# Turning normalised rows through DRAM and DVE's 32x32 transposes in place of PE's transposes, in a four-layer attention and MLP kernel

## Chip, cores and metric

The kernel runs on one core of one Trainium2 chip. The metric is the device time of one execution in microseconds, lower is better. The kernel before takes 2529.15 us, the median of three runs (2528.08 to 2529.36).

## The reference

Four blocks run one after the other on 2048 rows of 576 numbers, all float32: attention A, MLP B, attention A, MLP B, with the same weights both times. Each adds its result to the rows, and each begins with a LayerNorm of the rows.

```python
def _A_ref(x, wqkv, w_phi, wo):
    q, k, v = ...                      # x @ wqkv, in 32 heads of 18
    phi_q = concatenate([softmax(q @ w_phi), softmax(-(q @ w_phi))])
    phi_k = concatenate([softmax(k @ w_phi), softmax(-(k @ w_phi))])
    kv = einsum("bhsf,bhsd->bhfd", phi_k, v); z = einsum("bhsf->bhf", phi_k)
    num = einsum("bhqf,bhfd->bhqd", phi_q, kv)
    den = einsum("bhqf,bhf->bhq", phi_q, z)[..., None] + 1e-6
    return (num / den) ... @ wo

def _B_ref(x, w1, b1, w2, b2):         # w1: 576 x 4608, w2: 4608 x 576
    h = relu(x @ w1 + b1)
    return (h * h) @ w2 + b2

x = x + _A_ref(layernorm(x), ...)
x = x + _B_ref(layernorm(x), ...)
x = x + _A_ref(layernorm(x), ...)
x = x + _B_ref(layernorm(x), ...)
```

## The kernel before

**Blocks and tiles.** The 2048 rows are cut into four blocks (`NB`) of 512 rows (`TB`), and a block into four tiles of 128 rows (`NT`). The matmuls contract over the 576 features, so the normalised rows are needed with the features on the partitions: four chunks of 128 features (`KC`) and a rest of 64 (`DT`). Float32 values are split into a high part in fp32r and the difference, so that a product is three passes: an array `xh` holds the high part, `xl` the low part of the four full chunks, and the fifth chunk of `xh` holds the high part of the rest on one half of the partitions and its low part on the other half.

**The MLP loop.** `g_mlp` (L759) runs one block through the MLP: for each of 36 slices `f` of 128 hidden features, `hidden(f)` (L808) is 14 matmuls into the PSUM bank `h` (L824), `square(f)` (L826) makes ReLU and square on ACT (L829, L830) and splits the result on DVE (L833, L834), and `second(f - 1)` (L852) is 15 matmuls into five accumulators (L849, L841). There is one bank `h`, so `hidden(f + 1)` can only start when the ReLU of `f` has read it. In the first block of the first layer the weights are split and stored to DRAM (`fresh`, L784 to L797); in the other seven blocks they are loaded in split form, 640 KB (L787) and 576 KB (L799) for each `f`, into two buffers each. So a load of `f + 1` is issued when the matmuls of `f - 1` have let go of its buffer.

**What is woven in.** `g_mlp` yields after each `hidden` and each `second`, and `weave` (L92) then runs one slot of a `Plan` (L101): the attention of the next block, and in the first layer also keys and values of the block just finished. `plan.put(turn, depth, ...)` gives slot `round(2 * turn) + 1`, so whole turns lie behind a `second`, half turns behind a `hidden`; within a slot the larger depth comes first. After the first two `hidden`, slots 2 and 3 follow one another with nothing between them, behind `second(0)`.

**The norm.** `Norm` (L327) works on a tile `t` in steps: `stats` (L353, on DVE, and the inverse root on GpSimd), `scale` (L365: two DVE instructions, 512 and 64 columns, into `xn` and `xd`; in the attention of a block `then` also adds a bias to the rows and stores them to `xm`, L693 and L694), `turn` (L377: four PE transposes into a PSUM bank at L386, then ACT copies the high part at L387 and DVE makes the low part at L388), and `rest` (L390: for two tiles together two PE transposes of the 64 columns, L395, and an ACT and a DVE instruction, L396 and L397). `plan_norm` (L696) puts these steps into a plan. It is called in `plan_attend` (at L755), six times in all, and in `plan_keys` (at L1349), three times, all in the first layer. The opening, the barrier at the start of a layer and `between` the layers use `Norm` with steps of their own.

**Who orders what.** The instructions of PE, ACT, DVE and GpSimd run in the order of the program text (L1131 and L1386, `ordered`). SP, which issues every DMA, is not in that list: the framework orders its queue by its own estimate of when each DMA is ready. Whatever the order, SP issues one after the other, and a DMA that waits holds those behind it.

Of the kernel before, what the change touches and what calls it, by code (L numbers as in the profile page):

```python
# [7 lines left out]
F32 = mybir.dt.float32  # L8
F32R = mybir.dt.float32r
AF = mybir.ActivationFunctionType  # L10
ALU = mybir.AluOpType
AX = mybir.AxisListType

P = 128
TB = 512
NT = TB // P
# [5 lines left out]
def layers_kernel(  # L22
# [18 lines left out]
    nc = tc.nc  # L41
    S, D = x_in.shape[1], x_in.shape[2]
# [3 lines left out]
    out = out.rearrange("o s d -> (o s) d")  # L46
    NB = S // TB
    NF = F // P
    KC = D // P
    DT = D - KC * P  # L50
# [13 lines left out]
    sb = ctx.enter_context(tc.tile_pool(name="sb", bufs=2))  # L64
    ps_w = ctx.enter_context(tc.tile_pool(name="ps_w", bufs=2, space=bass.MemoryType.PSUM))
    ps_a = ctx.enter_context(tc.tile_pool(name="ps_a", bufs=1, space=bass.MemoryType.PSUM))
    dram = ctx.enter_context(tc.tile_pool(name="dram", bufs=1, space=bass.MemoryType.DRAM))

    xs = [[dram.tile([P, D], F32, name=f"xs{b}_{t}") for t in range(NT)] for b in range(NB)]
    xm = [[dram.tile([P, D], F32, name=f"xm{b}_{t}") for t in range(NT)] for b in range(NB)]  # L70
    xth = [dram.tile([P, NC * TB], F32, name=f"xth{b}") for b in range(NB)]
    xtl = [dram.tile([P, KC * TB], F32, name=f"xtl{b}") for b in range(NB)]
    dense1 = [dram.tile([P, 2 * NC * P], F32, name=f"dw1_{f}") for f in range(NF)]
# [6 lines left out]
    def wtile(name):  # L80
        n = len(spare["tags"])
        spare["i"] += 1
        i = spare["i"] % (n + 2)
        if i < n:
            return ps_a.tile([P, TB], F32, tag=spare["tags"][i], name=name)
        return ps_w.tile([P, TB], F32, tag="w", name=name)
# [14 lines left out]
    class Plan:  # L101

        def __init__(self):
            self.at = {}
# [64 lines left out]
    class Fold:  # L169
# [38 lines left out]
        def turn(self, k):  # L208
            c, i = divmod(k, 3)
            if i == 0:  # L210
                self.folds[c] = sb.tile([P, 2 * D], F32R, tag="wraw" if c in (2, 3) else "hb", name=f"ff{c}")
            w, n = gw[self.batches[i][0][1]], len(self.batches[i])
            pt = wtile(f"fp{c}_{i}")
            for j, (h, g) in enumerate(self.batches[i]):
                a = h * D + g * GW
                nc.tensor.transpose(pt[:w, j * P : (j + 1) * P], self.raws[c][:, a : a + w], ident)
            wt = self.wts[k] = sb.tile([GW, TB], F32, tag="ft", name=f"ft{c}_{i}", bufs=4)
            if i == 0:
                nc.vector.tensor_copy(wt[:w, : n * P], pt[:w, : n * P])
            else:  # L220
                nc.scalar.activation(wt[:w, : n * P], pt[:w, : n * P], AF.Copy)
# [82 lines left out]
    def asked(which, name, tags=TAGS_A):  # L304

        pair, calls = [], []

        def ask(half, k):
            if k == 0:
                pair.append(piece_tiles(f"{name}{which}{half}", tags))  # L310
            for d, piece in moved(which, half, k, pair[half][k]):
                nc.sync.dma_start(piece, d)

        return pair, [lambda half=half, k=k: ask(half, k) for half in range(2) for k in range(2)]
# [8 lines left out]
    def xt_tiles(name):  # L323
        return {"h": sb.tile([P, NC, TB], F32R, tag="xh", name=f"{name}h"),
                "l": sb.tile([P, KC, TB], F32R, tag="xl", name=f"{name}l")}

    class Norm:  # L327
# [37 lines left out]
        def scale(self, t):  # L365
            name = self.name
            x, (mv, rstd) = self.x.pop(t), self.stat.pop(t)
            if self.xd is None:
                self.xd = sb.tile([P, NT, DT], F32, tag="xd", name=f"{name}e", bufs=1)
            xn = sb.tile([P, KC * P], F32, tag="xn", name=f"{name}n{t}")  # L370
            nc.vector.tensor_scalar(xn, x[:, : KC * P], mv[:, 0:1], rstd, op0=ALU.subtract, op1=ALU.mult)
            nc.vector.tensor_scalar(self.xd[:, t], x[:, KC * P :], mv[:, 0:1], rstd, op0=ALU.subtract, op1=ALU.mult)
            if self.then:
                self.then(t, x)
            self.xn[t] = xn
# [14 lines left out]
        def rest(self, h):  # L390
            xh = self.dst["h"]
            rows = slice(h * TB // 2, (h + 1) * TB // 2)
            pt = wtile(f"{self.name}p{NT}{h}")
            for i in range(NT // 2):
                nc.tensor.transpose(pt[:DT, i * P : (i + 1) * P], self.xd[:, h * NT // 2 + i], ident)  # L395
            nc.scalar.activation(xh[:DT, KC, rows], pt[:DT, : TB // 2], AF.Copy)  # L396
            nc.vector.tensor_sub(xh[DT:, KC, rows], pt[:DT, : TB // 2], xh[:DT, KC, rows].bitcast(F32))  # L397

    XT = (("h", xth, 0, KC // 2), ("l", xtl, 0, KC // 2), ("h", xth, KC // 2, NC), ("l", xtl, KC // 2, KC))

    def xt_part(b, x, i):
        n, d, c0, c1 = XT[i]
        return d[b][:, c0 * TB : c1 * TB], x[n][:, c0:c1].rearrange("p c n -> p (c n)").bitcast(F32)

    def spill(b, x, parts=range(4)):
        for i in parts:
            d, piece = xt_part(b, x, i)
            nc.sync.dma_start(d, piece)
# [44 lines left out]
    def make_raw(x, t, pair, name):  # L453
        raw = new_raw(t, name)
        for half in range(2):
            half_raw(x, t, pair, half, raw, name)
        return raw
# [21 lines left out]
    def exponents(raw, name):  # L479
        mm = peaks(raw, name)  # L480
        e = new_e(name)
        for s in range(2):
            difference(raw, mm, e, s, nc.vector)
        return e
# [8 lines left out]
    def totals(e, r):  # L493
        exponential(e)
        normalisers(e, r)
# [197 lines left out]
            nc.vector.tensor_add(x, x, b2t)  # L693
            nc.sync.dma_start(xm[self.b][t], x)  # L694

    def plan_norm(plan, norm, x_of, stats, scales, turns, rests, late=()):  # L696
        for t in range(NT):
            plan.put(stats[t], 0, lambda t=t: norm.stats(t, x_of(t)))
            plan.put(scales[t], 1, norm.scale, t)
            plan.put(turns[t], -1 if t in late else 2, norm.turn, t)  # L700
        for h in range(2):
            plan.put(rests[h], 2, norm.rest, h)
# [35 lines left out]
    def plan_attend(plan, at, gap, layer, b, raws, dst, name, o, queries=None):  # L738

        out = Out(layer, b, [], name)  # L740
        out.pair, calls = o
        if queries:
            for t in range(NT):
                plan.put(at + gap * t, 0, queries, t)
            at += 1
        for n, call in enumerate(calls):
            plan.put(at + n, 9, call)
        at = plan_queries(plan, at, gap, layer, raws, [], out.ph, name) + 1
        for i in range(2 * NG):
            plan.put(at + i / 2, 0, out.turn, i)  # L750
            plan.put(at + (i + 1) / 2, 1, out.times, i)
        at += NG + 1
        for t in range(NT):
            plan.put(at + t - 1, 9, out.load, t)
        plan_norm(plan, Norm(dst, f"{name}n", out.keep), out.project, [at + t for t in range(NT)],  # L755
                  [at + 1, at + 2, at + 4, at + 5], [at + 4 + t for t in range(NT)], [at + 5, at + 7])


# [585 lines left out]
    def plan_keys(plan, prev_rows, last, keep):  # L1344

        pb, done = prev_rows
        m = f"1_{pb}"
        xk, es, ks, vts = {}, {}, {}, {}
        plan_norm(plan, Norm(xk, f"n{m}"), lambda t: done[t], (0, 0, 1, 2), (1, 1, 2, 3), (2, 3, 4, 4.5), (3, 5), (3,))  # L1349
        (vw, vcalls), (kw, kcalls) = asked("v", f"w{m}"), asked("k", f"w{m}", TAGS_C)  # L1350
        for n in range(4):
            plan.put(8 + n if last else 2 + n / 2, 9, vcalls[n])
            plan.put(n / 2, 9, kcalls[n])
        if not last:
            for n in range(4):
                plan.put(5 + n / 2, -1, lambda n=n: spill(pb, xk, [n]))

        def keys(t):
            ks[t] = make_raw(xk, t, kw, f"k{m}k")

        def values(t):
            vts[t] = make_v(xk, t, vw, f"v{m}")

        def soft1(t):
            es[t] = exponents(ks.pop(t), f"k{m}K{t}")

        def soft2(t):
            r = sb.tile([P, 2, H], F32, tag="r", name=f"k{m}K{t}r")
            totals(es[t], r)
            scaled(es[t], r)  # L1370

        def add(t):
            kv_tile(1, vts.pop(t), es.pop(t), f"kv{m}_{t}")

        for t in range(NT):
            plan.put(4 + t, 0, keys, t)
            plan.put(5 + t, 1, soft1, t)
            plan.put(6 + t, 2, soft2, t)
            if not last:
                plan.put(4.5 + t, 0, values, t)  # L1380
                plan.put(8.5 + t // 2 * 2, 3, add, t)
        if last:
            keep.update(x=xk, es=es, v=vw, k=kw)
        return 11.5
# [25 lines left out]
```

## Time and profile before

| | |
|---|---|
| median of three runs | 2529.15 us |
| the profiled execution: its time, its span | 2530.61 us, 2528.9 us |
| ACT busy | 741.9 us, 29% of the span |
| granted TensorE clock | 1.000 |
| DMA moved | 505.48 MB, 200 GB/s over the span |
| DMAs issued by SP for the weights in split form (L787, L799) | 252 of each |

The span runs from the first to the last instruction. "Busy" is the time that an engine works on an instruction; a wait is not busy. The chain of waits follows the work that ended last back to the start, at each step to what released it, and so shows who set the end. The trace of the profile can be asked for stretches of time, for lines of the kernel and for who waited for whom. Of DMAs it shows when SP issued them and what waited for them; the share of the 16 DMA engines that was busy is given for a stretch.

### The profile page before, as it was taken

Reading aid. Unit: us, or ns where it says so; the run is one execution under the profiler, and the core shown is the slowest. Engines: PE = TensorE matmul, PEld = TensorE weight load, DVE = VectorE, ACT = ScalarE, POOL = GpSimd, SP = SyncE. Lnnn points to the kernel's source line nnn. Section 1 sums busy time; section 2 is a strip of 40 time slices with the busy share of each in tenths; the row PEclk is TensorE's granted clock in tenths of the full one; section 3 lists DMA queues with packets and bytes.
Section 4 is the critical chain, followed back from the end, with each engine's and each line's share of the span. In section 5 each row is a group of like instructions: output and inputs, shape, how many; then the busy total and the mean of one; then the engine's idle time right before and its main releaser. Section 6 shows DMA issues by size and latency. Waiting matters only on the chain.

```text
span 2528.9 us, 37324 instructions
## 1 busy us (share of the span) xinstructions
PE 2512.7 (99%) x15300; PEld 2215.4 (88%) x15300; DVE 1166.8 (46%) x1986; ACT 741.9 (29%) x1268; POOL 113.4 (4%) x275
## 2 busy tenths in 40 slices
PE   9999999999999999999999999999999999999999
PEld 8998888888888988888888988888888888888887
DVE  6887955434634446345113775332353326332112
ACT  5544443322222222223223332222222222222221
POOL 4302000000000000000000010000000000000000
PEclk9999999999999999999999999999999999999999
DMA  9514887867647576484665345457544665456565
GB/s 318 174 53 138 288 280 259 309 216 265 214 148 261 179 262 213 147 272 147 196 198 168 115 142 189 152 192 258 183 161 155 221 231 164 148 187 230 195 193 174
DMA packets 161288, 505.48 MB, mean 200 GB/s; under 512 B 21350, under 2 KB 49798, under 8 KB 161118
## 3 DMA queue, kind: packets, MB, share of 16 engines
q1 hardware_dynamic: 161118, 503.10, 59.8%
q8 instruction: 121, 1.98, 0.3%
q14 instruction: 49, 0.40, 0.0%
HBM read 418.39 MB, written 84.64 MB: 199 GB/s over the span
## 4 chain that ended last, share of the span: by engine, by line
PE 97%; DMA 1%; DVE 1%; ACT 0%; issue 0%; SPq 0%; DVEq 0%; ACTq 0%
PE m_1ph L824 9%; PE m_3ph L824 9%; PE m_0ph L824 9%; PE m_2ph L824 9%; PE m_1acc L849 7%; PE m_3acc L849 7%; PE m_2acc L849 7%; PE m_0acc L849 7%; PE m_1acc L841 2%; PE m_3acc L841 2%; PE m_2acc L841 2%; PE m_0acc L841 2%; PE a_2po L686 1%; PE a_0po L686 1%; PE kvp L527 1%; PE a_3po L686 1%
## 5 line engine op out<-in xcount | busy, mean ns | idle before, releaser
L824 PE MATMUL m_2ph<-a_2nh,m_2h 128*128 128x512 f32 x720 | 225.4, 395 | 2.1 <-DMA m_2h<-dw 2.1
L824 PE MATMUL m_0ph<-a_0nh,m_0h 128*128 128x512 f32 x720 | 226.3, 396 | 0.2 <-DMA m_0h<-dw 0.2
L849 PE MATMUL m_3acc<-m_3s,m_3hb 128*128 128x448 f32 x864 | 189.7, 367 | 0.3 <-DVE m_3hb L833 0.3
L849 PE MATMUL m_0acc<-m_0s,m_0hb 128*128 128x448 f32 x864 | 189.9, 368 | 0.0
L849 PE MATMUL m_1acc<-m_1s,m_1hb 128*128 128x448 f32 x864 | 189.4, 367 | 0.3 <-PE m_1ph L824 0.3
L849 PE MATMUL m_2acc<-m_2s,m_2hb 128*128 128x448 f32 x864 | 189.6, 367 | 0.0
L849 PEld LDWEIGHTS m_1acc<-m_1s,m_1hb 128*128 128x128 f32 x864 | 161.5, 188 | 18.2 <-PE m_1ph L824 0.5
L833 DVE CAST m_2hb<-m_2hr 128x512 fp32r<-128x512 f32 x72 | 30.8, 427 | 317.8 <-ACT m_2hr L830 317.4
L849 PEld LDWEIGHTS m_3acc<-m_3s,m_3hb 128*128 128x128 f32 x864 | 161.2, 188 | 17.8 <-PE m_3ph L824 0.5
L849 PEld LDWEIGHTS m_2acc<-m_2s,m_2hb 128*128 128x128 f32 x864 | 160.7, 188 | 16.1
L849 PEld LDWEIGHTS m_0acc<-m_0s,m_0hb 128*128 128x128 f32 x864 | 160.3, 188 | 15.6
L824 PEld LDWEIGHTS m_2ph<-a_2nh,m_2h 128*128 128x128 f32 x720 | 135.3, 188 | 32.8 <-issue 2.5
L824 PEld LDWEIGHTS m_0ph<-a_0nh,m_0h 128*128 128x128 f32 x720 | 135.3, 188 | 30.5 <-issue 0.6
L833 DVE CAST m_1hb<-m_1hr 128x512 fp32r<-128x512 f32 x72 | 30.7, 427 | 269.2 <-ACT m_1hr L830 269.2
L829 ACT ACTIVATE m_2hr<-m_2ph,b1t 128x512 f32<-128x512 f32 x72 | 49.6, 689 | 353.7 <-PE m_2ph L824 353.7
L833 DVE CAST m_0hb<-m_0hr 128x512 fp32r<-128x512 f32 x72 | 30.8, 427 | 260.8 <-ACT m_0hr L830 255.2
L829 ACT ACTIVATE m_0hr<-m_0ph,b1t 128x512 f32<-128x512 f32 x72 | 49.6, 689 | 334.3 <-PE m_0ph L824 334.3
L829 ACT ACTIVATE m_1hr<-m_1ph,b1t 128x512 f32<-128x512 f32 x72 | 49.6, 689 | 323.2 <-PE m_1ph L824 323.2
L829 ACT ACTIVATE m_3hr<-m_3ph,b1t 128x512 f32<-128x512 f32 x72 | 49.6, 689 | 240.3 <-PE m_3ph L824 240.3
L824 PE MATMUL m_3ph<-t0onh,m_3h 128*128 128x512 f32 (+1 forms) x380 | 113.3, 385 | 0.7 <-ACT t0onh L387 0.5
L833 DVE CAST m_3hb<-m_3hr 128x512 fp32r<-128x512 f32 x72 | 30.7, 426 | 180.5 <-ACT m_3hr L830 180.5
L824 PE MATMUL m_1ph<-t1onh,m_1h 128*128 128x512 f32 (+1 forms) x380 | 113.2, 385 | 0.6 <-ACT t1onh L387 0.5
(1934 smaller groups left out, 5618.8 us busy)
## 6 DMA issues: line engine op xcount, KB each, us to landing
m_2h<-dw SPq DMA_DIRECT2D x72, 640.0 KB
m_0h<-dw SPq DMA_DIRECT2D x72, 640.0 KB
m_1h<-dw SPq DMA_DIRECT2D x72, 640.0 KB
m_2s<-dw SPq DMA_DIRECT2D x72, 576.0 KB
m_0s<-dw SPq DMA_DIRECT2D x72, 576.0 KB
m_1s<-dw SPq DMA_DIRECT2D x72, 576.0 KB
dw<-m_3h SPq DMA_DIRECT2D x36, 640.0 KB
m_3h<-dw SPq DMA_DIRECT2D x36, 640.0 KB
```

What stands on the lines that cost most here:

```text
L527: nc.tensor.matmul(po[32 * q : 32 * q + 32, :, j], vt[:, h * VW : h * VW + 32], e[:, :, h * DH : (h + 1) * DH], start=not stay, stop=True, ...
L686: nc.tensor.matmul(pt[:, :HP], a, m[:w, g], start=(g == 0 and k == 0), stop=(g == NG - 1 and k == 2))
L824: nc.tensor.matmul(ph[:, cols], a, m, start=(k == 0), stop=(k == 3 * KC + 1))
L829: nc.scalar.activation(hr, ph, AF.Relu, bias=b1t[:, f : f + 1])
L833: nc.vector.tensor_copy(hh, hr)
L841: nc.tensor.matmul(acc[KC], a, m, start=(f == 0 and k == 0), stop=(f == NF - 1 and k == 2))
L849: nc.tensor.matmul(acc[t][:, :R], a[:, rows], m, start=(f == 0 and k == 0), stop=(f == NF - 1 and k == 2))
```

## The change

Both calls of `plan_norm` get a new class, `StoredNorm`, in place of `Norm`, and `plan_norm` puts one more step, `fetch`. `scale` normalises into a row tile of its own with the blocks of 32 columns in another order, and stores it to DRAM (`xr`). `fetch` reads it back with six DMAs, four for the 512 columns and two for the 64, so that each 32x32 block lies where its transpose belongs. `turn` then transposes all blocks with one DVE instruction in place, and ACT and DVE make the high and the low part from SBUF. `rest` does the same for the 64 columns of two tiles. `fetch` stands half a turn behind `scale` in `plan_attend`; in `plan_keys` the times of `stats` and `scale` are earlier than before and `fetch` has times of its own.

```diff
+    xr = [dram.tile([TB, D], F32, name=f"xr{b}") for b in range(NB)]
...
+    class StoredNorm(Norm):
...
+        def scale(self, t):
+            x, (mv, rstd) = self.x.pop(t), self.stat.pop(t)
+            row = sb.tile([P, D], F32, tag="qk", name=f"{self.name}r{t}", bufs=5)
+            args = dict(scalar1=mv[:, 0:1], scalar2=rstd, op0=ALU.subtract, op1=ALU.mult)
+            nc.vector.tensor_scalar(row[:, : KC * P].rearrange("p (a b c) -> p b a c", a=KC, b=KC),
+                                    x[:, : KC * P].rearrange("p (b a c) -> p b a c", a=KC, b=KC), **args)
+            nc.vector.tensor_scalar(row[:, KC * P :], x[:, KC * P :], **args)
+            if self.then:
+                self.then(t, x)
+            nc.sync.dma_start(xr[self.b][t * P : (t + 1) * P], row)
+
+        def fetch(self, t):
+            if self.xd is None:
+                self.xd = sb.tile([P, TB // 2], F32, tag="xd", name=f"{self.name}e", bufs=1)
+            rows = xr[self.b][t * P : (t + 1) * P].rearrange("(g r) f -> r g f", r=32)
+            xn = self.xn[t] = sb.tile([P, KC * P], F32, tag="xn", name=f"{self.name}n{t}")
+            for a in range(KC):
+                part = slice(32 * a, 32 * a + 32)
+                nc.sync.dma_start(xn[part].rearrange("p (g f) -> p g f", g=KC), rows[:, :, a * P : (a + 1) * P])
+            for a in range(DT // 32):
+                to = t * 2 // NT * DT + 32 * a
+                tail = self.xd[to : to + 32, t % 2 * P : (t % 2 + 1) * P]
+                at = KC * P + 32 * a
+                nc.sync.dma_start(tail.rearrange("p (g f) -> p g f", g=KC), rows[:, :, at : at + 32])
+
+        def turn(self, t):
...
+            nc.vector.transpose(xn, xn)
+            src = xn.rearrange("p (g b r) -> p b g r", g=KC, b=KC)
+            hi, lo = (z[:, :KC, rows].rearrange("p b (g r) -> p b g r", g=KC) for z in (dst["h"], dst["l"]))
+            nc.scalar.activation(hi, src, AF.Copy)
+            nc.vector.tensor_sub(lo, src, hi.bitcast(F32))
+
+        def rest(self, h):
+            xh = self.dst["h"]
+            rows = slice(h * TB // 2, (h + 1) * TB // 2)
+            own, far = (slice(i * DT, (i + 1) * DT) for i in (h, 1 - h))
+            xd = self.xd[own]
+            nc.vector.transpose(xd, xd)
+            nc.scalar.activation(xh[own, KC, rows], xd, AF.Copy)
+            nc.vector.tensor_sub(xh[far, KC, rows], xd, xh[own, KC, rows].bitcast(F32))
...
-    def plan_norm(plan, norm, x_of, stats, scales, turns, rests, late=()):
+    def plan_norm(plan, norm, x_of, stats, scales, turns, rests, late=(), fetches=None):
...
             plan.put(scales[t], 1, norm.scale, t)
+            plan.put(fetches[t] if fetches else scales[t] + 0.5, 9, norm.fetch, t)
             plan.put(turns[t], -1 if t in late else 2, norm.turn, t)
...
-        plan_norm(plan, Norm(dst, f"{name}n", out.keep), out.project, [at + t for t in range(NT)],
+        plan_norm(plan, StoredNorm(dst, f"{name}n", b, out.keep), out.project, [at + t for t in range(NT)],
                   [at + 1, at + 2, at + 4, at + 5], [at + 4 + t for t in range(NT)], [at + 5, at + 7])
...
-        plan_norm(plan, Norm(xk, f"n{m}"), lambda t: done[t], (0, 0, 1, 2), (1, 1, 2, 3), (2, 3, 4, 4.5), (3, 5), (3,))
+        plan_norm(plan, StoredNorm(xk, f"n{m}", pb), lambda t: done[t], (0, 0, 0.5, 1), (0.5, 0.5, 1, 1.5),
+                  (2, 3, 4, 4.5), (3, 5), (3,), (1, 1, 2.5, 3.5))
```

More of the change, by code (lines that the diff above doesn't have):

```diff
@@ L397, in rest, with __init__ @@
             nc.vector.tensor_sub(xh[DT:, KC, rows], pt[:DT, : TB // 2], xh[:DT, KC, rows].bitcast(F32))
+    class StoredNorm(Norm):
+        def __init__(self, dst, name, b, then=None):
+            super().__init__(dst, name, then)
+            self.b = b
+        def scale(self, t):
[22 more added lines that the diff above has]
+        def turn(self, t):
+            xn, dst = self.xn.pop(t), self.dst
+            if t == 0:
+                dst.update(xt_tiles(self.name))
+            rows = slice(t * P, (t + 1) * P)
+            nc.vector.transpose(xn, xn)
[11 more added lines that the diff above has]
+            nc.vector.tensor_sub(xh[far, KC, rows], xd, xh[own, KC, rows].bitcast(F32))
```

## The prediction

> **What bounds the kernel.** I read the page first: busy time, the DMA queues, the chain.
>
> ```profile
> PE 2512.7 (99%) x15300; PEld 2215.4 (88%) x15300; DVE 1166.8 (46%) x1986; ACT 741.9 (29%) x1268; POOL 113.4 (4%) x275
> ...
> q1 hardware_dynamic: 161118, 503.10, 59.8%
> ...
> PE 97%; DMA 1%; DVE 1%; ACT 0%; issue 0%; SPq 0%; DVEq 0%; ACTq 0%
> ```
>
> PE sets the end: it makes 97% of the chain. DVE is busy 46% of the span and the DMA engines 60%. "Busy" may hide waits, so next the waits of PE from 240 us (behind the opening and most of the first barrier) to the end, in us, times, longest; the eight rows of that answer sum to 4.3 us (the first, the seventh and the last are shown), and DMA ended two of them:
>
> ```profile
> PE m_2ph L824 <- DMA m_2h<-dw: 2.1, 1, 2.1
> ...
> PE m_0ph L824 <- DMA m_0h<-dw: 0.2, 1, 0.2
> PE m_1ph L824 <- DVE t1onh L397: 0.2, 1, 0.2
> ```
>
> So a PE instruction taken away is time taken away, as long as nothing new makes PE wait.
>
> **What the transposes cost on the path.** First the count, from the windows 245 to 1360 us (layer 0) and 1490 to 2529 us (layer 1), which leave out the opening, the barriers and `between`; the first pair of rows is for L386, the second for L395 (length, PE busy and count, weight loads, clock, DMA share, GB/s):
>
> ```profile
> 245.00:1360.00 1115.00, 14.36 (x96) 11.91 (x96) 1.00 0.67 226
> 1490.00:2529.00 1039.00, 7.18 (x48) 5.95 (x48) 1.00 0.59 192
> ```
>
> ```profile
> 245.00:1360.00 1115.00, 4.58 (x24) 2.64 (x24) 1.00 0.67 226
> 1490.00:2529.00 1039.00, 2.29 (x12) 1.33 (x12) 1.00 0.59 192
> ```
>
> That is 96 + 48 = 144 in 36 turns and 24 + 12 = 36 in 18 rests. The busy sums here (21.54 and 6.87 us) overlap with the neighbours, so the price is read from the chain, in a stretch of the first block (start, us, what), beside the same loop without turns a little later:
>
> ```profile
> 409.53 2.44 PE m_3acc L849 x12
> ...
> 412.66 0.44 PE a_2np L386 x4
> 413.09 3.22 PE m_3ph L824 x14
> 416.31 2.44 PE m_3acc L849 x12
> ...
> 419.44 0.43 PE a_2np L386 x4
> 419.88 0.22 PE a_2np L395 x2
> ...
> 423.36 2.46 PE m_3acc L849 x12
> ```
>
> ```profile
> 450.01 2.46 PE m_3acc L849 x12
> ...
> 456.39 2.44 PE m_3acc L849 x12
> ```
>
> A turn takes 0.44 us of the chain and a rest 0.22. The loop's period agrees: 456.39 - 450.01 = 6.38 us without, 416.31 - 409.53 = 6.78 with a turn, 423.36 - 416.31 = 7.05 with both. The change removes 36 x 0.44 + 18 x 0.22 = 15.8 + 4.0 = **19.8 us** of PE.
>
> One alone lasts longer than its share of the chain:
>
> ```profile
> L386 PE MATMUL a_2np<-ident,a_2nn x32: 270/272/273, 412.5 to 2264.9; 128*128 128x128 f32 x32
> ```
>
> The Trainium skill, "TensorE: Matmul & The Clock Gate", Part 4 (PE-mode transpose), gives about 275 ns for one transpose inside a kernel; the 272 ns here agree, and a sum by 0.275 us would be 180 x 0.275 = 49.5 us. I take the chain: what overlaps can't be saved.
>
> **What it adds on DVE and ACT.** Per tile one 32x32 transpose of 128x512, per two tiles one of 64x256. The trace has none; its nearest rows of these shapes, in the first block's attention (count, busy us, mean ns):
>
> ```profile
> L834 DVE TENSOR_TENSOR m_3hb<-m_3hr,m_3hb 128x512 fp32r<-128x512 f32 x10 | 6.9, 692 | 0.3
> ...
> L371 DVE TENSOR_SCALAR a_2nn<-a_2x,a_2nm,a_2nd 128x512 f32<-128x512 f32 x4 | 2.2, 542 | 0.0
> ...
> L397 DVE TENSOR_TENSOR a_2nh<-a_2np,a_2nh 64x256 fp32r<-64x256 f32 x2 | 0.8, 418 | 0.1
> ```
>
> The large one costs 0.54 to 0.69 us; I take the dearer row, an estimate of 36 x 0.69 + 18 x 0.42 = 32 us. DVE goes from 1166.8 to about 1200 us, 47%: off the path. The reordered `scale` lies between the same two rows, 36 x 0.15 = 5 us at worst, also beside PE. The high and low parts are the same instructions from SBUF instead of PSUM; at nothing, since ACT has 71% of the span free.
>
> **What it adds on DMA.** Per tile 288 KB out and 288 KB back, 36 x 0.59 = 21 MB. The page's queue moved 503 MB in 59.8% of the span; at that rate it is 2.5 points more. In bytes it is hidden nearly everywhere.
>
> **What it adds on SP, and who is behind it.** Per tile seven DMAs more, 252 in all, and one wait: the first `fetch` has to wait until the store has landed. Behind it in the queue stand the weight loads L787 and L799, and for those PE waits. The trace has such a wait already: the loads of `xm` (L911) wait for an earlier store of the same 288 KB, here in layer 1.
>
> ```profile
> 1632.33 0.46 SPq L694 DMA_DIRECT2D xm<-a_0x  x1
> 1637.15 0.32 SPq L911 DMA_DIRECT2D m_1x<-xm  x1
> 1638.66 0.32 SPq L787 DMA_DIRECT2D m_1h<-dw  x1
> ...
> 1642.71 0.32 SPq L694 DMA_DIRECT2D xm<-a_0x  x1
> 1646.57 0.32 SPq L911 DMA_DIRECT2D m_1x<-xm  x1
> ```
>
> ```profile
> SPq L911 <- DMA xm<-a_0x: 16.3, 6, 4.3
> ```
>
> A store is gone 4.8 and 3.9 us after its issue; SP stood up to 4.3 us for it, and PE has no wait there. Six issues at 0.32 to 0.46 us are 1.9 to 2.8 us more. So in the attention parts (24 tiles) the trip is some 4.8 + 2.8 us, then the landing of the last load; from `fetch` to `turn` the plan leaves 1.5 to 2.5 periods of at least 6.38 us. DVE does not wait there, and I put these tiles at nothing; if that cover is gone, the price is in the third rival.
>
> The tight place is the first tile in `plan_keys`: `scale` in slot 2, `turn` in slot 5. Its old course, in the chain and on DVE, in the first such block:
>
> ```profile
> 498.30 8.28 DMA m_2h<-dw
> ...
> 513.30 0.43 PE n_3p L386 x4
> 513.74 3.27 PE m_2ph L824 x14
> 517.01 2.44 PE m_2acc L849 x12
> ```
>
> ```profile
> 506.55 0.31 DVE L372 TENSOR_SCALAR n_3e<-m_3x,n_3m,n_3d 128x64 f32<-128x64 f32 x1
> ```
>
> ```profile
> 501.00:508.00 7.00, 4.94 (x24) 4.02 (x23) 4.63 (x13) 1.32 (x2) 1.66 (x4) 1.00 0.88 310
> 508.00:515.00 7.00, 7.00 (x36) 5.99 (x35) 2.52 (x6) 1.92 (x3) 0.79 (x2) 1.00 0.80 298
> ```
>
> The row is ready at 506.9. With the store at 3.9 to 8.3 us (the last from the DMA in the chain, at this place), six issues of 1.9 to 2.8 and a landing of again 3.9 to 8.3, the rows are back between 516.6 and 526.3. Behind the waiting transpose on DVE stand the splits of `square(3)`, behind the waiting copy on ACT its ReLU, and for that ReLU `hidden(4)` waits, since there is one bank `h`. `hidden(3)` starts at 513.3 without the turn, `second(2)` ends 3.3 + 3.1 us later, at 519.7: by then transpose, copy and ReLU, each 0.6 to 0.7 us, have to be through, 2.0 us after the rows are back. The wait of PE is nothing at the early end and 526.3 + 2.0 - 519.7 = 8.6 us at the late one. With DMA shares of 0.88 and 0.80 I take a store of 6 us and loads like the store of the quieter stretch, 4.8: back at 506.9 + 6 + 2.4 + 4.8 = 520.1, a wait of some 2.4 us. In the other two such blocks PE has no wait for a DMA above 0.2 us in the list at the top, so their queues are shorter: half a microsecond each, between nothing and the same 8.6. A gain from the trip itself is excluded, since it takes nothing off SP or the DMA engines. **Cost: 3.4 us.**
>
> **Sum.** The profiled execution took 2530.61 us, its span and 1.7 us around it: 2530.61 - 19.8 + 3.4 = 2514.2. It lay 1.46 us above the median of 2529.15, so **2512.8 us** is the forecast, 0.65% faster; 0.2% (5 us, about what a measurement of this kernel can tell from no change) is well below it.
>
> **The rivals.**
>
> *Late turns (chance 0.18).* In each of the three key blocks the first turn comes half of the worst case late, 4.3 us, because queue after queue is busier than I read: 13 us of the gain go, 2529.15 - 19.8 + 13 = 2522. For it: the DMA piece of 8.28 us in the chain lies just there. Against: PE's list of waits has only one of that kind, 2.1 us.
>
> *Nothing is freed (0.08).* The change doesn't do what it says: where the transposes stood, PE waits for the same neighbours, and the time stays at 2529. Against: the periods of 6.38, 6.78 and 7.05 us differ by just the transposes.
>
> *SP holds the weights (0.08), slower.* SP stands 4.8 + 2.8 = 7.6 us per tile. A load of L787 is issued when a `hidden` ends and is needed one and a half periods, 9.6 us, later; if it lands in 5 us, about the 4.8 of the store, it has 4.6 to spare, and one that falls due as SP begins to stand is 3.0 late. With two loads in 6.38 us one falls in these 3.0 us, 1.5 late on the mean; in all 12 key tiles and half of the 24 others that is 24 x 1.5 = 36 us, and 2529.15 - 19.8 + 36 = 2545. It decides from 0.55 us per tile on (19.8 / 36). For it: SP is ordered by an estimate, and the wait may stand ahead of a load that is due. Against: the 4.3 us above, which cost nothing. The Trainium skill, "VectorE: DVE Perf Modes", Rules for kernel authors, sides with this rival: it sends a 128x128 transpose to TensorE wherever a PSUM destination will do, and leaves to DVE the 32x32 blocks. Its reason, a DVE that can't cross 32 partitions, is just what the trip makes up for; no run so far shows the price.
>
> *The full duration counts (0.02).* PE gives back 272 ns per transpose, 49 us: 2480. The chain speaks against it.
>
> **How the numbers follow.** My forecast has 0.64. Low end: no new wait, 2509.4, and a microsecond for the price of a turn: 2508. High end: late turns and a little more, 2525. Outside lie most of "nothing freed", "SP holds" and the last, some 0.18. Faster by over 0.2%: 0.63 of mine, 0.14 of the late turns, 0.02: 0.79. Within: 0.04 of the late turns and 0.08: 0.12. Slower: 0.08 of SP and 0.01 of mine, 0.09.
>
> **What would show it.** Right: L386 and L395 left only for the opening, the barriers and `between`; PE busy about 20 us less at the same length of the other groups; period 6.4 us where turns lie; SP waits for a DMA of `xr` of some 2 to 5 us; DVE transposes of 0.5 to 0.7 us; a short wait of PE at `hidden(4)` of the first key block. Wrong: waits of L824 or L849 for DMAs of `dw` in many tiles (SP holds), or waits at L824 for ACT behind DVE transposes that wait for DMA in the attention parts too.

## The result, and the profile after

The changed kernel takes 2570.91 us (median of 4 runs, 2567.59 to 2571.84) beside 2529.26 for the kernel before (4 runs): 1.0163 times the time, 95% interval 1.0146 to 1.0181, so 41.7 us slower where 16.3 us faster were forecast. Its profiled execution took 2567.59 us, with a span of 2565.9: 37.0 more than before.

The page of the changed kernel: busy time, the DMA queue, the chain.

```profile
PE 2509.5 (98%) x15120; PEld 2206.3 (86%) x15120; DVE 1198.4 (47%) x2040; ACT 747.1 (29%) x1268; POOL 114.5 (4%) x275
...
q1 hardware_dynamic: 197406, 524.35, 61.3%
...
PE 92%; DMA 4%; DVE 2%; ACT 1%; SPq 1%; issue 0%; POOL 0%; DVEq 0%; ACTq 0%
```

The 180 transposes are gone (15,300 to 15,120 instructions), DVE has grown by 31.6 us and the DMA share by 1.5 points, all about as worked out. DVE's two kinds of transpose, one row of each, in the changed kernel (count, then ns least, median and most, then first and last start):

```profile
L436 DVE STREAM_TRANSPOSE a_2nn<-a_2nn x8: 704/705/711, 414.7 to 2299.7; 128x512 f32<-128x512 f32 x8
```

```profile
L447 DVE STREAM_TRANSPOSE a_2ne<-a_2ne x4: 429/436/442, 423.1 to 2301.8; 64x256 f32<-64x256 f32 x4
```

But PE is busy only 3.2 us less, and DMA has gone from 1% to 4% of the chain. The waits of PE from 240 us to the end (us, times, longest):

```profile
PE m_0ph L877 <- DMA m_0h<-dw: 13.1, 3, 6.2
PE m_2ph L877 <- DMA m_2h<-dw: 11.8, 3, 5.0
PE m_1ph L877 <- DMA m_1h<-dw: 11.7, 3, 6.1
PE m_3ph L877 <- DMA m_3h<-dw: 2.0, 2, 1.7
PE m_2acc L894 <- DVE a_0nl L440: 1.5, 1, 1.5
PE m_0acc L894 <- DVE a_1nl L440: 1.4, 1, 1.4
...
```

L877 is `hidden` (L824 before). 38.6 us are waits for weight tiles, eleven in number; before it was 2.3 us. This is the sign that the prediction had named for "SP holds the weights". One of them in full, in the second key block: first SP's queue (start, duration, what), then PE (the wait stands in brackets).

```profile
835.43 0.32 SPq L852 DMA_DIRECT2D m_0s<-dw  x1
837.63 4.06 SPq L415 DMA_DIRECT2D xr<-n_2r  x3
841.79 1.84 SPq L424 DMA_DIRECT2D n_2n<-xr  x4
843.73 0.85 SPq L429 DMA_DIRECT2D n_2e<-xr  x2
844.62 1.86 SPq L424 DMA_DIRECT2D n_2n<-xr  x4
846.52 0.98 SPq L429 DMA_DIRECT2D n_2e<-xr  x2
847.60 0.38 SPq L415 DMA_DIRECT2D xr<-n_2r  x1
848.09 0.38 SPq L852 DMA_DIRECT2D m_0s<-dw  x1
848.51 0.44 SPq L840 DMA_DIRECT2D m_0h<-dw  x1
```

```profile
847.32 0.87 PE L894 MATMUL m_0acc<-m_0hb,m_0s 128*128 128x512 f32 x3
854.39 0.76 PE L877 MATMUL m_0ph<-a_0nh,m_0h 128*128 128x512 f32 x1 [6.21 <-DMA m_0h<-dw]
```

Three stores, which take until 841.69 since two of them wait for their `scale`, twelve fetches, another store and a tile of `m_0s` stand ahead of the weight tile. It is issued at 848.51; PE could have used it at 848.18 (854.39 less 6.21). The buffer that it goes into was free from 838.62, when the `hidden` that last read it ended, so it is issued some 10 us late: 3.1 us of these go to the last stores, 5.5 to the twelve fetches. It then needs 5.9 us to land.

Behind the wait the matmuls are slow. Stretches of the changed kernel (length; busy us and count of PE, weight loads, DVE, ACT, GpSimd; granted clock; DMA share; GB/s):

```profile
835.00:848.00 13.00, 13.00 (x60) 10.89 (x58) 9.34 (x25) 3.16 (x5) 4.15 (x16) 1.00 0.60 194
848.00:854.00 6.00, 0.18 (x1) 0.00 (x0) 3.02 (x6) 1.05 (x2) 0.00 (x0) 0.79 0.97 303
854.00:860.00 6.00, 5.61 (x17) 4.52 (x18) 0.00 (x0) 0.28 (x1) 0.00 (x0) 0.64 0.90 249
...
2020.00:2034.00 14.00, 11.90 (x55) 9.93 (x54) 4.51 (x8) 3.69 (x6) 0.00 (x0) 1.00 0.84 279
```

After 6.2 us without work PE gets a clock of 0.64 on the mean of 6 us, and in the 5.61 us in which it is busy 17 matmuls run where 26 would fit at the pace of the first row. After a wait of 2.1 us (last row) the clock stays at 1.00. The Trainium skill, "TensorE: Matmul & The Clock Gate", Why this matters for your kernels, asks for no idle gap above about 3 us, since one idle window brings the clock to half; the 6.2 and the 2.1 us here agree with it; waits in other runs that do not are in the last section. The prediction had priced every wait of PE at its own length only.

The balance of the span, from the rows above, those of before and run e1 below (all without the trip, PE busy 2493.7): transposes removed -19.0 (2493.7 - 2512.7), the same 15,120 instructions at a lower clock +15.8 (2509.5 - 2493.7), waits +39.4 (43.7 in the whole list less 4.3): +36.2 of the 37.0.

### The profile page after: what moved, and what is told of

Its sections match the earlier page's. It is cut to its first block, busy times and chain, and to the rows that moved or that the text cites. A ratio compares the mean times of both kernels' runs of the same rounds, so it can differ in the third digit from the quotient of the medians.

```text
span 2565.9 us, 37442 instructions
## 1 busy us (share of the span) xinstructions
PE 2509.5 (98%) x15120; PEld 2206.3 (86%) x15120; DVE 1198.4 (47%) x2040; ACT 747.1 (29%) x1268; POOL 114.5 (4%) x275
## 2 busy tenths in 40 slices
DMA packets 197580, 526.75 MB, mean 205 GB/s; under 512 B 34599, under 2 KB 81479, under 8 KB 197407
## 4 chain that ended last, share of the span: by engine, by line
PE 92%; DMA 4%; DVE 2%; ACT 1%; SPq 1%; issue 0%; POOL 0%; DVEq 0%; ACTq 0%
PE m_2ph L877 9%; PE m_0ph L877 9%; PE m_1ph L877 9%; PE m_3ph L877 9%; PE m_1acc L902 7%; PE m_3acc L902 6%; PE m_2acc L902 6%; PE m_0acc L902 6%; PE m_2acc L894 2%; PE m_1acc L894 2%; PE m_3acc L894 2%; PE m_0acc L894 2%; PE a_2po L738 1%; PE a_0po L738 1%; DMA m_1h<-dw 1%; DMA m_0h<-dw 1%
## 5 line engine op out<-in xcount | busy, mean ns | idle before, releaser
L877 PE MATMUL m_2ph<-a_2nh,m_2h 128*128 128x512 f32 x720 | 230.6, 402 | 11.8 <-DMA m_2h<-dw 11.8
L877 PE MATMUL m_0ph<-a_0nh,m_0h 128*128 128x512 f32 x720 | 228.5, 399 | 13.1 <-DMA m_0h<-dw 13.1
L877 PEld LDWEIGHTS m_2ph<-a_2nh,m_2h 128*128 128x128 f32 x720 | 138.7, 193 | 44.8 <-issue 8.1
L877 PEld LDWEIGHTS m_0ph<-a_0nh,m_0h 128*128 128x128 f32 x720 | 137.0, 190 | 45.0 <-issue 9.1
L877 PE MATMUL m_1ph<-a_1nh,m_1h 128*128 128x512 f32 x360 | 115.4, 402 | 9.9 <-DMA m_1h<-dw 9.9
L877 PE MATMUL m_2ph<-a_2nl,m_2h 128*128 128x512 f32 x288 | 115.3, 400 | 0.0
L877 PE MATMUL m_1ph<-t1onh,m_1h 128*128 128x512 f32 (+1 forms) x380 | 112.9, 384 | 2.4 <-DMA m_1h<-dw 1.8
```

The source lines that it names most:

```text
L877: nc.tensor.matmul(ph[:, cols], a, m, start=(k == 0), stop=(k == 3 * KC + 1))
```

## The experiments

Each ratio is to the kernel before, measured beside the run, with a 95% interval. "The trip" is the store and the six fetches of a tile. In the cuts of code "-" is the changed kernel and "+" the run, in e11 and e16 the kernel before and the run.

**e1, no trip: what the rest of the change is worth.**

```
- nc.sync.dma_start(xr[...], row)            # the store
- the six loads of fetch()
+ scale() writes into xn and xd; key parts at the old plan times
```

> This leaves the store and the six loads out: scale writes its reordered rows straight into the tile that DVE transposes, at the times of the old plan, so that part of the values end up in the wrong places. Queue theory (weight loads stand behind the trip's DMAs in SP's queue): PE loses its 180 transposes and nothing else, 2529.2 - 19.8 = 2509.5 us, no wait of PE for dw over 2.1 us, clock 1.000. DMA load theory (the 512-byte and 128-byte packets crowd the DMA engines): the same 2509.5. DVE theory (the transposes on DVE hold up the splits behind them): stays above 2540.

2513.44 us, ratio 0.9934 (0.9919 to 0.9949). The page and the longest waits of PE:

```profile
PE 2493.7 (99%) x15120; PEld 2197.4 (88%) x15120; DVE 1200.8 (48%) x2040; ACT 746.6 (30%) x1268; POOL 113.3 (5%) x275
```

```profile
PE m_2py L976 <- ACT m_2yt L954: 1.1, 1, 1.1
PE m_0py L976 <- ACT m_0yt L954: 1.1, 1, 1.1
PE m_2ph L870 <- DMA m_2h<-dw: 0.9, 1, 0.9
```

The forecast's two prices for PE and DVE hold: PE gives back 19.0 us and DVE's transposes cost nothing but two waits of 1.1 us at the end of an MLP. So the trip, with the plan times that it needs in the key parts, costs 57.5 us.

**e2 and e3: the change in the attention parts alone, in the key parts alone.**

```
e2, plan_keys:    - StoredNorm(xk, f"n{m}", pb)   + Norm(xk, f"n{m}"), old plan times
e3, plan_attend:  - StoredNorm(dst, ..., b, out.keep)   + Norm(dst, ..., out.keep)
```

> The trip in the six attention parts only; keys as before. Queue theory: PE saves 6 x 2.2 = 13.2 us, and the waits stay that stand at the start of an MLP (4.4, 1.5, 4.8, 1.4, 3.8 us in layer 0) and in layer 1 (5.8 us in all), with about 5 us of lowered clock: 2529 - 13 + 22 + 5 = 2543. DMA load theory: waits only where the DMA engines are at 0.8 or more, that is in the key parts, so here 2516 to 2522.

> The trip in the three key parts only; attention as before. Queue theory: PE saves 3 x 2.2 = 6.6 us; the waits in the key parts stay (2.4, 5.0, 6.2, 6.1 us) and 10 us of lowered clock: 2529 - 7 + 20 + 10 = 2552. DMA load theory: nearly the whole loss is here, 2565 or more.

e2: 2546.42, ratio 1.0065 (1.0050 to 1.0080); e3: 2540.45, 1.0040 (1.0026 to 1.0053). Both parts cost by themselves: where 13.2 and 6.6 us less of PE would have given 2516.6 and 2523.2, 30 and 17 us are lost. The two add up to 47 of the 57.5 us; the other 10 come only when both are there. The 2543 expected for e2 were near, the 2552 for e3 were 12 us too high: of the three waits of 5 to 6 us that the key parts have in the changed kernel only one came, of 7.6 us, in the first block. The waits of e2, none longer than 4.7 us, stand where one MLP ends and the next begins; that is where the second weight tile had stood ahead of the four `xs` stores, which wait for DVE, and now stands behind them. SP's queue at such a place (ahead of the wait of 4.4 us at 496 us), in the full change:

```profile
487.40 0.37 SPq L840 DMA_DIRECT2D m_2h<-dw  x1
492.71 1.98 SPq L975 DMA_DIRECT2D xs<-m_3x  x4
494.74 0.58 SPq L852 DMA_DIRECT2D m_2s<-dw  x1
495.37 0.72 SPq L840 DMA_DIRECT2D m_2h<-dw  x1
```

and of the kernel before, where the last of the first two tiles is issued at 488.34 and the stores follow:

```profile
488.34 0.32 SPq L787 DMA_DIRECT2D m_2h<-dw  x1
...
494.28 2.72 SPq L922 DMA_DIRECT2D xs<-m_3x  x4
```

The edit touches no weight load; the framework moved it.

**e4: the whole trip on GpSimd's queue.**

```
- nc.sync.dma_start(...)      + nc.gpsimd.dma_start(...)      # store and six loads
```

> All seven DMAs of a tile are issued by GpSimd instead of SP (in the key parts the first two fetches half a turn later, behind the last statistics, so that GpSimd's inverse roots do not stand behind them). Queue theory: SP is free again, the weight loads go out when their buffers do, 2509.5 plus up to 6 us of late turns: 2510 to 2516, no wait of PE for dw over 2.1 us. DMA load theory: the same bytes and packets, so the waits stay, 2560 or more. Rival within the queue theory: GpSimd is slower at issuing, turns come late, and PE waits for ACT and DVE instead of DMA: 2515 to 2540.

2573.98, ratio 1.0169 (1.0146 to 1.0191). Waits of PE:

```profile
PE m_0ph L877 <- ACT m_0hr L882: 9.4, 2, 6.6
PE m_0py L983 <- ACT m_0yt L961: 8.4, 1, 8.4
...
PE m_2ph L877 <- DMA m_2h<-dw: 0.8, 1, 0.8
```

The weights are in time, with the same bytes moved; so their lateness comes from SP's queue and not from the bytes. (The packets are fewer here, 171,082 for 197,580; e13 below has all of them.) But now the turns are late. A store is issued at 802.94, the tile's fetches follow on GpSimd from 810.13, and DVE stands 6.71 us until 817.87; ACT's copy of the high part and its `m_2yt` wait behind it, and PE for `m_2yt` (7.85 us, until 821.56). In most other places it is the ReLU that comes late. For this case I had expected 2515 to 2540.

**e5 and e9: the queue's entries without the bytes, and with them, the turns freed from the trip.**

```
e5:  + 16 bytes a row in each of the seven DMAs; DVE copies row to xn
e9:  - nc.vector.transpose(xn, xn) on the fetched tile    + on the row in SBUF
```

> The trip's seven DMAs per tile stay in SP's queue, in their order and with their waits, but move 16 bytes a row where they moved 2,304 (store) and 512 or 128 (fetches); the turn's source is copied from the scaled row by DVE, so that no turn waits for a DMA (values misplaced, DVE some 20 us busier). Theory of SP's queue: the weight loads still stand behind stores that wait for DVE and behind the issues, so PE waits for DMAs of dw remain near those of the changed kernel (35 of 44 us) and the clock drops with them: 2545 to 2570 us. Theory of DMA load (the trip's 21 MB and its small packets delay the weights): next to no bytes are left, 2513 to 2518 us, as without the trip.

> The whole trip with all its bytes, waits and order in SP's queue, but the turn reads the scaled row that is still in SBUF in place of the fetched tile (values misplaced): no turn waits for a fetch, and a fetch into xn waits for no turn, since nothing reads xn. The trip without bytes (run e5) kept 23.6 of the 57.5 us that the trip costs. Theory of the loop through DVE (a turn that waits for its fetch holds DVE, so the next scale and its store come late, and the weights behind that store): the other 34 us are this loop, and this kernel is near e5, 2535 to 2545 us. Theory of the bytes (the fetches' small packets keep the DMA engines busy, so that the weights issued after them land later): near the changed kernel, 2558 to 2572 us.

e5: 2537.01, ratio 1.0029 (1.0019 to 1.0040), between its two ranges; e9: 2569.37, 1.0151 (1.0135 to 1.0166). e9 shows that the loop through DVE isn't the cause: freed turns bring nothing as long as the weights are late. Between e5 and e9 lie 32 us, which look like the bytes. But their queues are not the same. e5 in the second key block has the weight tile ahead of all fetches:

```profile
832.64 1.32 SPq L416 DMA_DIRECT2D xr<-n_2r  x2
...
834.54 0.37 SPq L845 DMA_DIRECT2D m_0h<-dw  x1
835.84 0.32 SPq L431 DMA_DIRECT2D n_2f<-xr  x1
```

e9 has it behind three stores and twelve fetches, as the changed kernel. With other sizes and DVE's copies the framework's estimate gives another order, so this pair tells nothing of the bytes by itself.

**e13, e14, e16: the order alone.** All instructions and bytes of the changed kernel (e16: of the kernel before) stay.

```
+ with tc.high_priority(60):      # e14: 100
      nc.sync.dma_start(both1, dense1[f])     # and both2
```

> The changed kernel with the same instructions, DMAs and bytes; the only edit is a priority of 60 places for the weight loads (both1, both2) when the framework orders SP's queue. In its order the weight tile that stood behind twelve fetches of a key block stands ahead of them, and the second tile of an MLP ahead of the four xs stores. Theory of SP's order: most of the 39 us of PE waits and the clock's 17 us go; the turns may come later, 2518 to 2540 us. Theory of the bytes (weights land late whatever the order, as the trip's packets take the DMA engines): 2560 us and more.

> As e13 with a priority of 100 places: weight loads that wait for PE to give their buffer back now stand between the fetches of a tile and hold these. Theory of SP's order: the waits for weights go further down, but the turns of the key blocks wait for their fetches, 2525 to 2555 us, with PE waiting for DVE or ACT behind the turns in place of the weights. Theory of the bytes: 2560 us and more.

> The control: the kernel before with the same priority for its weight loads. It has 5.0 us of PE waits in all, 2.3 of them for weights: 2526 to 2530 us by every theory.

e13: 2570.00, ratio 1.0160 (1.0146 to 1.0174); e14: 2591.86, 1.0238 (1.0222 to 1.0254); the control e16: 2530.73, 1.0004 (0.9995 to 1.0013). Waits of PE in e13:

```profile
PE m_2ph L879 <- ACT m_2hr L884: 6.4, 1, 6.4
PE m_0py L985 <- ACT m_0yt L963: 5.7, 1, 5.7
PE m_1ph L879 <- ACT m_1hr L884: 5.5, 2, 3.8
PE m_0ph L879 <- ACT m_0hr L884: 5.4, 2, 3.8
PE m_2py L985 <- ACT m_2yt L963: 5.3, 1, 5.3
PE v_3pv L479 <- DMA w_3v1l<-kept_vl: 5.1, 1, 5.1
...
PE m_0ph L879 <- DMA m_0h<-dw: 0.7, 1, 0.7
```

The expectation came true by halves: the weights are in time, as the theory of the order said, and the time didn't move, as the theory of the bytes said, though not for its reason. At the second and third key block, where the changed kernel waits 6.2 and 6.1 us for weights, e13 has one wait of 1.7 and one of 1.8 us, both for ACT; all bytes and packets are there, so it is not they that make these tiles late. But now the trip stands behind the weights and the turns are late, and so are two tiles of the attention's weights (6.2 us of waits for `w_3v1l` and `w_3v1h`). e14, expected at 2525 to 2555, came out higher still, with waits of up to 10.4 us for the ReLU. In e13's DVE, for instance, the last turn of a block:

```profile
818.84 0.71 DVE L436 STREAM_TRANSPOSE a_0nn<-a_0nn 128x512 f32<-128x512 f32 x1 [4.13 <-DMA a_0nn<-xr]
```

PE's wait of 5.3 us (for `m_2yt`, which ACT makes behind this turn) ends at 822.54. The theory that only the order of SP's queue costs has fallen with this: no order tried lets one queue serve both.

**e6, e12, e18: other splits between queues.**

```
e6:   weight loads both1, both2 of later blocks   nc.sync -> nc.gpsimd
e12:  the stores to xr, xm and xs                 nc.sync -> nc.gpsimd
e18:  e2 with the six fetches                     nc.sync -> nc.scalar
```

> The changed kernel with one thing moved: the weight loads of the later blocks (both1, both2) are issued from GpSimd's queue, the trip stays on SP's with all its bytes. Theory of SP's queue: the trip no longer holds the weights; what is left is the removed PE work and whatever GpSimd's own waits cost the weights: 2514 to 2530 us, waits for dw below 10 us. Theory that the trip itself is late for its turns (as it was when all seven DMAs went to GpSimd): PE waits for ACT behind the turns, 2540 us and more. Theory of DMA load: weights late whatever the queue, 2545 us and more.

> The changed kernel with the three stores that wait for DVE (the scaled row, xm and xs) issued from GpSimd's queue; SP keeps all the loads, weights and fetches. If the weights were late because they stood behind stores that wait for DVE: SP now waits in the fetches alone, 2525 to 2545 us, and the waits at the start of an MLP (4.4, 4.8, 3.8 us) are gone. If the fetches hold SP as long by themselves (they wait for the store to land and for the xn buffer that a turn gives back): 2555 to 2575 us.

> The attention parts' four tiles by the trip as in e2 (2546.4 us), but the six fetches of a tile are issued from ACT's queue; the store stays on SP, the key parts on PE. In its order SP has the second weight tile of the second, third and fourth MLP ahead of the four xs stores. Theory of SP's queue: weights in time, and ACT bears 24 x 6 issues of some 0.4 us = 2.6 us a tile within the 5 us that a ReLU may be late: PE waits of 0 to 1 us at each border, 2516 to 2524 us, below e8. If ACT, which now waits for the store to land ahead of the fetch, holds the ReLU of square: waits for ACT m_hr, 2525 to 2545 us.

e6: 2631.03, ratio 1.0401 (1.0383 to 1.0418): on GpSimd the weights stand behind the norms' inverse roots, which wait for DVE (in the second key block GpSimd sat 9.98 us for `n_2m`, until 852.04, and issued a weight tile only then), and come later than ever. e12: 2558.94, 1.0115 (1.0101 to 1.0129): 12 us better than the full change, the 4.4 us at 496 gone, but the fetches hold SP as well, as the second of its ranges had it (SP stood up to 8.8 us for a store in the first key block, until 514.09). e18: 2569.09, 1.0156 (1.0142 to 1.0170), 23 us worse than e2. There ACT waits for the store, with the ReLU behind it (SP issued this store at 791.74, and PE had waited 4.30 us for the ReLU at 799.14):

```profile
795.63 1.76 ACTq L427 DMA_DIRECT2D a_0nn<-xr  x4
...
798.40 0.69 ACT L885 ACTIVATE m_2hr<-m_2ph,b1t 128x512 f32<-128x512 f32 x1 [9.26 <-DMA m_2h<-dw]
```

e6 and e18 missed alike: both texts name what already waits in the new queue, and price it far too low (2631 for at most 2530, 2569 for at most 2545). The Trainium skill, "DMA: Bandwidth & Descriptors", Where the ~2 us actually goes, says that a DMA's wait is done by the sequencer that issues it, before it is dispatched; e18's ReLU behind a fetch agrees.

**e7, e8, e10, e15, e17: fewer tiles, more room.**

```
e7:   e3 with fetches at (1.5, 2, 3, 3.5), turns at (3, 3.5, 4, 4.5), rests at (3.5, 5)
e8:   attention parts: tiles 0, 1 and rest 0 by the trip; tiles 2, 3 and rest 1 by PE; keys by PE
e10:  e8, and in the key parts tiles 0, 1 (main blocks) by the trip
e15:  e10 with the priority of e13
e17:  e8, and tile 2 (main blocks) by the trip
```

> The trip in the key parts alone, with the fetches planned at 1.5, 2, 3, 3.5 (before: 1, 1, 2.5, 3.5) and turns at 3, 3.5, 4, 4.5 (before: 2, 3, 4, 4.5), rests at 3.5 and 5: a weight load falls between any two fetches, and no two tiles' twelve loads stand in a row. Theory of SP's queue: the one wait of 7.6 us at the first key block (two fetches and two stores in a row ahead of a weight tile) and its clock window go, leaving 2523 to 2530 us against 2540 with the trip in the keys alone. Theory that the trip is too late for its first turn (my forecast's term of 2.4 us per block): no gain from the spreading, 2535 to 2545 us.

> The trip for tiles 0 and 1 of the dense attention parts alone; tiles 2 and 3 and rest 1, which stand at the border to the next MLP, and the key parts are turned by PE. PE saves six blocks' 2 x 0.44 + 0.22 = 6.6 us. Theory that the loss of the attention parts lies at the start of an MLP, where the scale of the last tiles holds the store and the first weight loads behind it: 2522 to 2527 us, no wait for dw over 1 us at 496, 812 and 1128 us. Theory that any trip in the attention parts costs its share: half of what all four tiles cost, 2535 to 2540 us.

> Tiles 0 and 1 of the attention parts by the trip, as in e8, and tiles 0 and 1 of the key parts as well (their four main blocks alone; the rests of the key parts stay on PE): PE saves 6.6 us in the attention parts and 3 x 2 x 0.44 = 2.6 us in the key parts. Theory of SP's queue: four fetches where the whole key part had twenty-four hold the weights by at most 2 us more in each part, and most of it is hidden: 2519 to 2524 us against 2523.2 for e8. Theory that the first turn of the key part comes too late for PE (my forecast's 2.4 us a part): 2526 to 2531 us.

> e10 (tiles 0 and 1 by the trip in both kinds of part, 2528.5 us, profiled 2523.4 with two waits for weights of 4.4 us in all and one clock window in the first key block) with the priority of 60 places. Theory of SP's order: the 4.4 us and the window go: 2517 to 2522 us. If the waits in the first key block come from DMA load there: no change, 2523 to 2529 us.

> Tiles 0, 1 and 2 of the attention parts by the trip (tile 2 its four main blocks alone; tile 3 and rest 1 on PE), the key parts by PE: 0.44 us for six more turns is 2.6 us of PE less than in e8, 2520.6 us if the third tile finds room. In its order of SP's queue the second weight tile of the second MLP stands behind the four xs stores, as it did with four tiles (a wait of 4.6 us and a clock window there), and ahead of them at the next border: one such border costs some 6 us, 2526 to 2529 us. If every border pays as with four tiles, 2535 us and more.

| run | us (median) | ratio, interval | waits of PE that are left |
|---|---|---|---|
| e7 | 2536.38 | 1.0026, 1.0017 to 1.0035 | weights 6.5 us (one of 4.2, with a lower clock behind it), 3 x 1.2 for late turns |
| e8 | 2523.23 | 0.9975, 0.9965 to 0.9984 | weights 2.2 us, longest 1.2 |
| e10 | 2528.48 | 0.9994, 0.9985 to 1.0003 | weights 4.4 us, longest 3.1 |
| e15 | 2537.68 | 1.0032, 1.0021 to 1.0043 | none for weights above 0.4; for `scale` on DVE 5.7 (behind a late turn), 1.6, 1.2; 1.1, 1.1, 0.6 for late rests |
| e17 | 2528.11 | 0.9993, 0.9984 to 1.0002 | weights 5.3 us, longest 4.4 |

e8 and e17 fell in the ranges of the theory that they were to test; e7, e10 and e15 came out 6, 4.5 and 16 us above theirs. e8 is faster than both kernels: its first row of waits and its page show why.

```profile
PE m_2ph L914 <- DMA m_2h<-dw: 2.2, 3, 1.2
```

```profile
PE 2506.4 (99%) x15240; PEld 2209.1 (88%) x15240; DVE 1177.2 (47%) x2004; ACT 743.2 (29%) x1268; POOL 113.2 (4%) x275
```

PE gives back 6.3 us and no wait, the longest being 1.2 us, lowers the clock, which is 1.00 in the whole run. It leaves out just the tiles next to the start of the next MLP. e17 takes one of them back; the weight tile at the border goes behind the `xs` stores, 4.4 us, as its queue order had said, and the gain is gone. e15 is the e13 story once more, in its third form: weights ahead, so the trip comes late, and on DVE the `scale` of a later tile stands behind a turn that waited 4.55 us for its fetch (until 525.95).

**e11: what idle time costs PE.**

```
+ for _ in range(wait.get(f, 0) if layer == 0 and b == 1 else 0):
+     nc.vector.tensor_copy(hh, hr)      # 15 to 28 times, ten values of f
```

> The kernel before, with DVE's copy into m_1hb repeated 15 to 28 times in ten steps of the last block of layer 0, where nothing else is woven in: PE sits idle in each of them by the repetitions over 12 times 0.43 us, so by 1.3, 2.1, 2.6, 3.0, 3.4, 3.9, 4.3, 5.2, 6.0 and 6.9 us, 38.7 us in all. If idle time costs no more than itself: 2568 us, granted clock 1.00 throughout. If the clock halves after an idle of some 2.4 us and more, as the traces of the changed kernel have it, for 3.4 or 6.8 us each time: eight windows with 1.7 to 3.4 us of lost work in each, 2582 to 2595 us.

2605.77, ratio 1.0298 (1.0284 to 1.0312). The page, the waits and two stretches, ahead of the idles and around the first, of 2.44 us:

```profile
PE 2536.5 (97%) x15300; PEld 2231.0 (86%) x15300; DVE 1255.6 (48%) x2196; ACT 741.5 (28%) x1268; POOL 113.0 (4%) x275
```

```profile
PE m_1acc L852 <- DVE m_1hb L836: 52.1, 10, 8.5
```

```profile
1160.00:1226.00 66.00, 66.00 (x324) 57.39 (x323) 33.27 (x49) 17.88 (x26) 0.00 (x0) 1.00 0.52 166
1226.00:1243.00 17.00, 14.56 (x59) 11.80 (x58) 8.38 (x20) 2.64 (x4) 0.00 (x0) 0.90 0.42 141
```

The idles came out longer than worked out (52.1 us for 38.7): 15 copies gave 2.44 us and 28 gave 8.45, which is 0.46 us a copy, so the slack was some 10 copies and not 12. What matters: the same 15,300 instructions took 23.8 us more of PE (2536.5 less 2512.7), 46% on top of the idle time, as in the changed kernel 15.8 on top of 38.6 (41%). Here nothing else is different, so the clock's part is shown.

## Why the prediction was wrong, step by step

- **What PE gives back: right.** 19.8 us forecast, 19.0 in e1.
- **DVE and ACT: right.** The transposes take 0.70 and 0.44 us (0.69 and 0.42 assumed), DVE 31.6 us in all (32). The rule of the Trainium skill ("VectorE: DVE Perf Modes", Rules for kernel authors) that sends a 128x128 transpose to TensorE had the right side, but not by DVE's blocks: e1 has all of them and is faster; the trip that they need is dear.
- **DMA bytes: right in size**, 1.5 points of share for 2.5; e4 and e13 show that they are not what makes the weight tiles late.
- **"DVE does not wait there, and I put these tiles at nothing": the step that failed.** The 24 attention tiles alone lose 30 us (e2). The step looked at the turn, which was in time, and took for SP a wait of 4.3 us that cost nothing before. It did not ask in which order SP would stand: the framework ordered it anew, and a weight tile went behind the `xs` stores.
- **The key blocks: right place, wrong victim.** 3.4 us were set down for the turn of the first tile; what came late was the weight behind twelve fetches, with waits of 5.0, 6.2 and 6.1 us in the three blocks. Alone, the key parts cost 17 us (e3). The rival "late turns" is 2.9 us of waits in the changed kernel; such waits became large only where the trip was put behind something else (e4, e13, e14).
- **Left out: the clock.** 15.8 us, behind most of the longer waits.
- **The rival "SP holds the weights" (0.08, 2545)** had mechanism, sign and the view that would show it. Its price was 36 us of waits; 38.6 were measured. That the two are so near is in part luck: it counted 24 waits of 1.5 us behind holds of 7.6 us a tile, 4.8 of them for the store, and eleven waits came, of 3.5 us on the mean. In the changed kernel SP stood at most 1.9 us for a store (21 us in 24 waits), and 30.5 us in stores that waited for `scale` on DVE, a hold that the rival did not have. Of the 26 us by which it was too low 15.8 are the clock. It had far too little chance: what I held against it, that one wait of SP had cost nothing, was one case in a queue whose order was about to change.

What stays open: SP has several holds in the changed kernel that no run separated, the issue times, the waits for `scale` and those for the store. Its list of waits has also a few rows in which a DMA waits for one of another tile (two fetches at L429 for `m_2s`, 1.7 us); whether that costs anything was not tried. Nor was it tried why e2 and e3 together lose 10 us less than the whole. That a fetch can't start while a turn still holds its `xn` buffer of two was removed in e9 only, where the weights decided.

## What to carry to other kernels

A trip through DRAM is paid in a queue, not in bytes: some engine has to issue the loads and wait for the store, and what stands behind them in its queue is late. Before adding waiting DMAs to a queue that feeds the critical engine, list its entries with their due times in the new order, not in the old one, for a framework may re-order those that the edit doesn't touch; and add to the waits of PE, where they are of several us, some two fifths for the clock (41% in the changed kernel, 46% in e11). Where a change wins in some places and loses in others, take it only where the queue has room: half of this one's attention tiles gave 0.25%, the whole lost 1.6%.

## What was not expected of the hardware

Idle time of PE is dearer than itself, and the length of one wait does not decide alone. Behind a wait of 1.87 us in e6 (at 1970.4 us) the granted clock was 0.50 for 3.4 us; behind one of 3.57 us in e9 (at 1144.0 us) it stayed at 1.00 (the columns are those of the stretches above; first e6, then e9):

```profile
1972.40:1975.80 3.40, 3.40 (x9) 2.63 (x9) 0.00 (x0) 0.00 (x0) 0.00 (x0) 0.50 0.76 313
```

```profile
1147.60:1151.00 3.40, 3.40 (x15) 2.77 (x16) 0.00 (x0) 0.00 (x0) 0.00 (x0) 1.00 1.01 415
```

Between these it went both ways: 2.34 us (e18) and 2.44 us (e11) lowered the clock, 2.35 us (e7) and 2.77 us (e4) did not. So the "about 3 us" of the Trainium skill, quoted with the result, is no sharp border here; what else decides stays open.

GpSimd needs 0.55 us for an issue where SP needs 0.32 to 0.48, and a store issued there landed after 3.5 to 6.7 us (median by tensor, e4).
